# Sliding-window attention followed by a two-matmul expert layer: from 768-token units to 256-token granules with half-array attention tiles

## The chip, the cores and the metric

The kernel runs on one core of one Trainium2 chip. The metric is the device time of one execution in microseconds, taken over repeated runs. A profile of one execution goes with each kernel. Its span is about 2 us shorter than the time of the same run.

Engine names in the profile: PE is the matrix engine and PEld its weight loads, DVE the vector engine, ACT the scalar engine (activations), POOL the engine that issues most of the loads here, SP the one that issues the stores.

## The reference

```python
# q, k, v: [4, 8, 768, 64]; n_global = 8, n_local = 96
scores = (q @ k.transpose(0, 1, 3, 2)) / sqrt(64)
rel  = pos[:, None] - pos[None, :]
keep = (pos[None, :] < 8) | ((rel >= 0) & (rel < 96))       # 8 global keys, or the last 96
dist = where(is_global & ~is_local, 96.0, abs(rel))
scores = where(keep, scores - slopes[h] * dist, -1e9)
a = softmax(scores)
x = (a @ v) as [3072 tokens, 512]                           # 4 * 768 tokens, 8 heads * 64
h = x @ w_in                                                # w_in  [512, 2048]
g = s * relu(h)**2 + b
out = g @ w_out                                             # w_out [2048, 512], float32 out
```

The layer after the attention is called the expert below; `x @ w_in` is its first matmul and `g @ w_out` its second. Note that every query looks at its own 128-token block, the block before it, and 8 global keys, and at nothing else.

## The kernel before

The unit of work is a pair of heads over all 768 tokens of one batch entry: 16 units. Queries and keys are loaded with tokens on partitions and transposed on PE. Both heads of a pair share one full-array score matmul, which needs the queries padded with zeros; the eight global keys take two more score matmuls. The probabilities are then the *weights* of the AV matmuls, and V, with a column of ones beside it, streams through: 65 columns, the last of which is the softmax denominator.

```python
ps_sc = ctx.enter_context(tc.tile_pool(name="ps_sc", bufs=4, space=bass.MemoryType.PSUM))
ps_av = ctx.enter_context(tc.tile_pool(name="ps_av", bufs=2, space=bass.MemoryType.PSUM))
ps_h = ctx.enter_context(tc.tile_pool(name="ps_h", bufs=2, space=bass.MemoryType.PSUM))
# ... prologue(ip): two DMAs each for q, k, v of this head pair ...
        nc.gpsimd.memset(v_ex2[:, :, :, D : D + 1], 1.0)          # the ones column, on POOL
# ... scores of block t: 128 keys against two blocks of zero-padded queries, both heads (L298)
                    ps[:, 0:ncol],                                # ncol = 512
                    lhsT=kP[:, t * P : (t + 1) * P],
                    rhs=zq[:, t : t + (2 if ncol == 4 * P else 1), :],
# ... AV (L373): 480 of these, lhsT = 128x128 probabilities, rhs = 65 columns of V
                            nc.tensor.matmul(ps_pair[:, dr, :], lhsT=lhsT, rhs=rhs, ...)
                    nc.vector.reciprocal(rec[:], ps_pair[:, :, D : D + 1])
                    nc.vector.scalar_tensor_tensor(out=xn[...], in0=ps_pair[:, :, 0:D],
                        scalar=sqrt_s[:], in1=rec[:]..., op0=ALU.mult, op1=ALU.mult)
# ... at the end of a batch entry: x is transposed for the expert
    def x_transpose_stage(bb):
        for kc in range(KC):
            pt = ps_h.tile([P, SB * P], BF16, tag="psh")
            for tb in range(SB):
                nc.tensor.transpose(pt[:, tb * P : (tb + 1) * P], ...)          # L403
            nc.vector.tensor_copy(xT_all[kc][:, bb * S : (bb + 1) * S], pt[:])  # L408
# ... expert, first matmul (a batch entry behind), 384 tokens a PSUM bank
                ps = ps_h.tile([P, 512], F32, tag="psh")
                for kc in range(KC):
                    nc.tensor.matmul(ps[:, 0:clen], lhsT=w_in_bf[:, kc, ...],   # L420
                        rhs=xT_all[kc][:, tok0 + cs0 : tok0 + cs0 + clen], ...)
                nc.scalar.activation(gT_all[...], ps[:, 0:clen], ACT.Relu)      # L427
            nc.vector.tensor_tensor(gs, gs, gs, ALU.mult)                       # L433
# ... expert, second matmul: 512 columns of w_out (L441), add of b, store
```

The expert of a batch entry runs between the attention of the next one. So PE can do no expert work until the attention of all four head pairs of the first entry is through.

The softmax here doesn't subtract the row's maximum and nothing guards it: scores larger than these inputs give would overflow.

## Time and profile before

| | before |
|---|---|
| time | 287.1 us, median of the first three runs; 288.6 over all 15 |
| profiled span | 285.8 us |
| PE busy | 246.2 us (86%) |
| PE work by steady spacing (below) | 225.7 us |
| of it done in the first 57 us | 19.1 us |

The opening of the page, with its slice rows (each digit is one fortieth of the span, 7.1 us, in tenths of busy time), and the shares of the chain of work that ended last:

```profile
span 285.8 us, 4714 instructions
PE 246.2 (86%) x1787; PEld 137.1 (48%) x1808; DVE 160.8 (56%) x471; ACT 147.7 (52%) x299; POOL 88.4 (31%) x132
...
PE   0476087799999999799999997999999999999994
...
DMA  6999999999908696942929252400001111000111
...
PE 76%; POOL 7%; ACT 6%; DMA 5%; DVE 3%; issue 1%; ACTq 0%; POOLq 0%
```

PE is the bound, but not from the start: for eight slices (57 us) it is partly idle while the DMA engines, which carry the loads, stand at nine tenths. The chain's pieces in the first 60 us (start, length, what) show the reason:

```profile
40.02 3.92 DMA k_pair<-in_k_dram
44.08 0.80 PE ps_k L254 x6
...
55.83 2.04 PE ps L420 x12
```

The first expert matmul (L420) starts at 55.8 us. The windows view cuts the span at 57 us (columns: window in us, its length, then busy time and instruction count of PE, PEld, DVE, ACT and POOL, then the granted clock, the DMA share and GB/s):

```profile
0.00:57.00 57.00, 28.86 (x270) 18.71 (x275) 35.59 (x122) 39.31 (x82) 42.53 (x68) 0.88 1.51 135
57.00:286.00 229.00, 217.36 (x1518) 118.37 (x1533) 125.26 (x350) 108.36 (x219) 45.90 (x64) 1.00 0.46 55
```

The groups of instructions, kept apart by form (line, engine, operation, output and inputs, shapes, count | busy us, mean ns | idle time before them and what ended it):

```profile
L420 PE MATMUL ps<-xT,w_in_bf 128*128 128x384 bf16 x512 | 91.3, 325 | 1.7 <-ACT gT_all L427 1.2 <-ACT zq L276 0.4 <-DVE xT L408 0.2
L441 PE MATMUL po<-w_out_bf,gT_all 128*128 128x512 bf16 x376 | 86.3, 379 | 0.4
L427 ACT ACTIVATE gT_all<-ps 128x384 bf16<-128x384 f32 x128 | 62.7, 490 | 42.6 <-PE ps L420 42.6
```

Two cautions on reading them. "128*128" is the part of the array that the matmul uses. And the mean of a matmul (325 ns) is its latency: matmuls overlap, so what counts for a busy PE is the distance from one start to the next. The steady distances in the traces are 216 ns for 512 columns, 162 for 384, 109 for 256, 55.5 for 128, and 30 for 65. "PE work" in this document is the number of matmuls of each form times these distances. In the first expert matmul every eighth start (57 of the 512 matmuls) comes 250 to 260 ns after the last instead of 162: a tile takes four matmuls, only two PSUM buffers (`ps_h`) are there, and so after each two tiles the next has to wait for a 490 ns ReLU. The waits view of PE's weight loads shows the same (line waited in, what for: total us, times, longest):

```profile
PEld L420 <- issue: 10.9, 61, 0.8
```

### The profile page before, as it was taken

The numbers are of one execution on the slowest core, as the hardware profiler recorded it, in microseconds if no ns is written. First come the engines' busy times: TensorE is split into PE (matmuls) and PEld (weight loads), VectorE is DVE, ScalarE is ACT, GpSimd is POOL, SyncE is SP. The second block draws the span as 40 slices with busy tenths as digits, with TensorE's granted clock in tenths as the row PEclk, the third lists the DMA queues.
The fourth block names the chain that finished last, engine by engine and source line by source line (L and its number), as shares of the span: only waits on it lengthen the run. The fifth ranks groups of instructions, "written<-read, shape, count | busy, mean of one in ns | idle before, by whom it ended". The sixth has DMA issues, their size and how long they took to land.

```text
span 285.8 us, 4714 instructions
## 1 busy us (share of the span) xinstructions
PE 246.2 (86%) x1787; PEld 137.1 (48%) x1808; DVE 160.8 (56%) x471; ACT 147.7 (52%) x299; POOL 88.4 (31%) x132
## 2 busy tenths in 40 slices
PE   0476087799999999799999997999999999999994
PEld 0253055455555554555554544655554555555441
DVE  4378357963649283975465656956392836333221
ACT  6888356673575142875680606865760503774000
POOL 9996568397605152503342020200000000000000
PEclk9999667999999999999999999999999999999999
DMA  6999999999908696942929252400001111000111
GB/s 40 120 118 149 177 161 138 175 173 107 92 1 59 103 104 105 78 28 17 69 17 104 75 64 76 28 2 0 2 0 73 40 73 39 0 0 2 73 73 73
DMA packets 81717, 20.22 MB, mean 71 GB/s; under 512 B 76064, under 2 KB 78112, under 8 KB 81696
## 3 DMA queue, kind: packets, MB, share of 16 engines
q0 software_dynamic: 77952, 13.64, 60.8%
q1 hardware_dynamic: 3744, 6.29, 5.9%
q8 instruction: 14, 0.23, 0.3%
q14 instruction: 7, 0.06, 0.1%
HBM read 27.26 MB, written 6.29 MB: 117 GB/s over the span
## 4 chain that ended last, share of the span: by engine, by line
PE 76%; POOL 7%; ACT 6%; DMA 5%; DVE 3%; issue 1%; ACTq 0%; POOLq 0%
PE ps L420 31%; PE po L441 29%; DMA k_pair<-in_k_dram 5%; PE ps L298 5%; PE ps_pair L373 4%; ACT pt L309 3%; POOL q_pair L228 3%; POOL k_pair L232 2%; PE psg L323 2%; POOL v_ex L238 2%; ACT zq L276 1%; PE ps_k L254 1%; PE pt L403 1%; PE ps_cs L195 1%; PE ps_q L262 1%
## 5 line engine op out<-in xcount | busy, mean ns | idle before, releaser
L420 PE MATMUL ps<-xT,w_in_bf 128*128 128x384 bf16 x512 | 91.3, 325 | 1.7 <-ACT gT_all L427 1.2
L441 PE MATMUL po<-w_out_bf,gT_all 128*128 128x512 bf16 x376 | 86.3, 379 | 0.4
L427 ACT ACTIVATE gT_all<-ps 128x384 bf16<-128x384 f32 x128 | 62.7, 490 | 42.6 <-PE ps L420 42.6
L309 ACT ACTIVATE pt<-ps 128x512 bf16<-128x512 f32 x96 | 46.2, 576 | 59.2 <-PE ps L298 54.9
L420 PEld LDWEIGHTS <-w_in_bf 128*128 128x128 bf16 x512 | 48.8, 96 | 39.4 <-issue 10.9
L433 DVE TENSOR_TENSOR gT_all<-gT_all 128x768 bf16<-128x768 bf16 x64 | 35.7, 558 | 43.3 <-ACT gT_all L427 42.9
L441 PEld LDWEIGHTS <-gT_all 128*128 128x128 bf16 x384 | 35.9, 98 | 39.1 <-DVE gT_all L433 0.2
L449 DVE TENSOR_TENSOR o_sb<-po,bvec_rep 128x512 f32<-128x512 f32 x24 | 16.5, 689 | 47.9 <-PE po L441 47.9
L238 POOL DMA_DIRECT2D v_ex<-in_v_dram x32 | 26.8, 862 | 31.8 <-issue 31.8
L232 POOL DMA_DIRECT2D k_pair<-in_k_dram x32 | 27.5, 862 | 27.4 <-PE ps L298 18.2
L312 DVE TENSOR_TENSOR pt<-pt,bmp 128x512 bf16<-128x512 bf16 x96 | 33.8, 394 | 1.8 <-ACT pt L309 1.5
L298 PE MATMUL ps<-zq,kP 128*128 128x512 bf16 (+1 forms) x84 | 29.6, 400 | 3.7 <-ACT zq L276 2.8
L384 DVE SCALAR_TENSOR_TENSOR xnat<-ps_pair,sqrt_s,rec 128x128 bf16<-128x128 f32 x96 | 30.8, 346 | 1.0
L373 PE MATMUL ps_pair<-v_ex,pt 128*128 128x65 bf16 x352 | 28.5, 198 | 3.0 <-DVE xnat L384 2.8
L373 PEld LDWEIGHTS <-pt 128*128 128x128 bf16 x352 | 23.0, 100 | 16.8 <-DVE xnat L384 8.6
L254 PE MATMUL ps_k<-ident_bf,k_pair 128*128 128x128 bf16 x96 | 12.1, 241 | 21.8 <-DMA k_pair<-in_k_dram 21.7
L228 POOL DMA_DIRECT2D q_pair<-in_q_dram x32 | 27.5, 866 | 0.7 <-PE ps_pair L373 0.4
L254 PEld LDWEIGHTS <-k_pair 128*128 128x128 bf16 x96 | 8.6, 107 | 28.2 <-issue 22.9
L331 ACT ACTIVATE pgt<-psg 128x512 bf16<-128x512 f32 x32 | 18.4, 651 | 1.1 <-PE psg L323 1.1
L373 PE MATMUL ps_pair<-v_ex,pgt 128*128 128x65 bf16 x128 | 18.7, 196 | 0.0
L383 DVE RECIPROCAL rec<-ps_pair 128x2 f32<-128x2 f32 x96 | 13.6, 160 | 6.4 <-PE ps_pair L373 5.9
L276 ACT COPY zq<-ps_q 64x768 bf16<-64x768 bf16 x16 | 12.7, 793 | 8.1 <-DVE zq L272 4.9
(42 smaller groups left out, 145.3 us busy)
## 6 DMA issues: line engine op xcount, KB each, us to landing
out_dram<-o_sb SPq DMA_DIRECT2D x24, 256.0 KB, 2.0
q_pair<-in_q_dram POOLq DMA_DIRECT2D x32, 96.0 KB, 3.7
k_pair<-in_k_dram POOLq DMA_DIRECT2D x32, 96.0 KB, 3.6
v_ex<-in_v_dram POOLq DMA_DIRECT2D x32, 96.0 KB, 3.6
w_in_bf<-in_moe_w_in_dram POOLq DMA_DIRECT2D x4, 512.0 KB, 8.1
w_out_bf<-in_moe_w_out_dram POOLq DMA_DIRECT2D x4, 512.0 KB, 8.6
s_bc<-in_moe_s_dram SPq DMA_DIRECT2D x1, 0.5 KB, 2.9
b_bc<-in_moe_b_dram SPq DMA_DIRECT2D x1, 0.5 KB, 3.5
```

The costliest lines, as they stand in the source:

```text
L228: nc.gpsimd.dma_start(q_pair[:, :, hi, :], q[bb, h0 + hi].rearrange("(sb p) d -> p sb d", p=P),)
L232: nc.gpsimd.dma_start(k_pair[:, :, hi, :], k[bb, h0 + hi].rearrange("(sb p) d -> p sb d", p=P),)
L238: nc.gpsimd.dma_start(v_ex2[:, :, hi, 0:D], v[bb, h0 + hi].rearrange("(sb p) d -> p sb d", p=P),)
L298: lambda t=t, ps=ps, ncol=ncol: nc.tensor.matmul(ps[:, 0:ncol], lhsT=kP[:, t * P : (t + 1) * P], rhs=zq[:, t : t + (2 if ncol == 4 * P els ...
L309: nc.scalar.activation(pt[:, 0:ncol], ps[:, 0:ncol], ACT.Exp, scale=QSCALE)
L312: nc.vector.tensor_tensor(pt[:, 0:ncol], pt[:, 0:ncol], bm[:, 0:ncol], ALU.mult)
L373: nc.tensor.matmul(ps_pair[:, dr, :], lhsT=lhsT, rhs=rhs, start=(i_mm == 0), stop=(i_mm == len(mms) - 1),)
L384: nc.vector.scalar_tensor_tensor(out=xn[:, r0 : r0 + 2, hh * D : (hh + 1) * D], in0=ps_pair[:, :, 0:D], scalar=sqrt_s[:], in1=rec[:].to_br ...
L420: nc.tensor.matmul(ps[:, 0:clen], lhsT=w_in_bf[:, kc, fc * P : (fc + 1) * P], rhs=xT_all[kc][:, tok0 + cs0 : tok0 + cs0 + clen], start=(kc ...
L427: nc.scalar.activation(gT_all[:, fc, cs0 : cs0 + clen], ps[:, 0:clen], ACT.Relu,)
L433: nc.vector.tensor_tensor(gs, gs, gs, ALU.mult)
L441: nc.tensor.matmul(po[:, 0:DM], lhsT=gT_all[:, fc, tb * P : (tb + 1) * P], rhs=w_out_bf[:, fc, :], start=(fc == 0), stop=(fc == FC - 1),)
```

## The change

The intent is to get PE to the expert earlier and to keep it there. It is a rewrite of the schedule; the diff is cut to the parts that matter.

- The unit is 256 tokens of a head pair (48 units; a "granule" is 256 tokens of all heads). Loads go by granule, so that the first granule's expert can start long before the batch entry is loaded.
- Scores and AV use half of the array per head. Scores use 64 rows (64\*128); AV uses 64 columns (128\*64) with V as the weights and the probabilities streaming, so that the result comes out as [head dim, tokens], which the expert needs: no transposes of x.
- The denominators are extra matmuls with a block of ones as weights; their reciprocal is exp(-ln(sum)) on ACT.
- The global keys are copied into the tile of the previous block's keys (`koff`, `voff`), so they need no matmul of their own.
- All eight PSUM banks form one pool; ReLU and square work on 512 columns.
- The order of the steps is fixed by hand: two units per step, first matmul of granule j−1, second of j−2.

```diff
-    ps_sc = ctx.enter_context(tc.tile_pool(name="ps_sc", bufs=4, space=bass.MemoryType.PSUM))
-    ps_av = ctx.enter_context(tc.tile_pool(name="ps_av", bufs=2, space=bass.MemoryType.PSUM))
-    ps_h = ctx.enter_context(tc.tile_pool(name="ps_h", bufs=2, space=bass.MemoryType.PSUM))
+    ps_all = ctx.enter_context(tc.tile_pool(name="ps_all", bufs=8, space=bass.MemoryType.PSUM))
+    ps_sc = ps_av = ps_h = ps_all
 ... loads, in this order
+    load_granule(0, 0)
+    load_granule(0, 1)
+    for i in range(4):
+        load_w_in(i, 4)
+    load_granule(0, 2)
+    for i in range(4):
+        load_w_out(i, 4)
 ... scores (L267)
-            mm_ops.append(lambda ...: nc.tensor.matmul(ps[:, 0:ncol],
-                    lhsT=kP[:, t * P : (t + 1) * P], rhs=zq[:, t : t + 2, :]))
+            for kt, kc0, qc0, oc in plan:           # 4 pairs of blocks, 3 in granule 0
+                for hi in range(2):
+                    r0 = hi * D
+                    nc.tensor.matmul(
+                        pss[hi][:, oc * P : (oc + 1) * P],
+                        lhsT=kt[r0 : r0 + D, kc0 : kc0 + P],
+                        rhs=t[r0 : r0 + D, qc0 : qc0 + P], start=True, stop=True)
 ... AV (L315), then the denominators (L328)
+                    for hi in range(2):
+                        nc.tensor.matmul(
+                            av[hi * D : (hi + 1) * D, i * P : (i + 1) * P],
+                            lhsT=vv, rhs=pts[hi][:, c * P : (c + 1) * P], ...)
+                    for hi in range(2):
+                        nc.tensor.matmul(
+                            av[hi * D : (hi + 1) * D, GT + i * P : GT + (i + 1) * P],
+                            lhsT=ones_bf[:, 0:D], rhs=pts[hi][:, c * P : (c + 1) * P], ...)
 ... norm, straight into xT
-                    nc.vector.reciprocal(rec[:], ps_pair[:, :, D : D + 1])
-                    nc.vector.scalar_tensor_tensor(...)
-    def x_transpose_stage(bb): ...
+            nc.scalar.activation(lg[:], av[:, GT : 2 * GT], ACT.Ln)               # L338
+            nc.scalar.activation(rc[:], lg[:], ACT.Exp, scale=-1.0)               # L340
+            nc.vector.tensor_tensor(xT[j][:, hp, :], av[:, 0:GT], rc[:], ALU.mult)  # L341
 ... first expert matmul (L354): two groups of 256 columns a bank, then one ReLU of 512 (L362)
 ... main loop
+    for s in range(0, NSTEP, 2):
+        ...                    # scores of units s+2, s+3; AV and ones of s, s+1
+        if 1 <= jm <= NJ:
+            for i in range(2):
+                moe_p1(jm - 1, 2 * qd + i)
+        if 2 <= jm:
+            moe_p2(jm - 2, qd // 2, 0)
+            moe_p2(jm - 2, qd // 2, 1)
+        if s + 4 < NU:
+            run_T2(s + 4)      # transposes of q and k
+        if 1 <= jm <= NJ:
+            for i in range(2, 4):
+                moe_p1(jm - 1, 2 * qd + i)
```

## The prediction

> **What bounds it now.** The page gives PE 86% busy, and the chain of waits is 76% PE: 31% the first expert matmul (L420), 29% the second (L441). The 40-slice view splits the run. For the first 57 us PE is 51% busy (28.9 us, windows view), while DMA slices stand at 9 and POOL issues 0.86 us per load; then PE is 217 of 229 us busy. Busy time flatters PE, so I used spacing between matmul starts (trace): L441 216 ns (512 columns), L420 162 ns (384 columns), with every fourth about 251 ns, since two PSUM buffers make PE wait for the 490 ns ReLU; attention-times-V (65 columns) 30 ns; 128-column transposes 55 ns. Summed at those steady rates, PE needs 83 (second) + 83 (first) + 26 (scores) + 14 (AV) + 16 (transposes) + 3.5 (bias) = about 226 us. The other 60 us is loading (about 35), ReLU waits (about 8), and attention chains and batch ends (about 17).
>
> **What changes.** The unit becomes 256 tokens instead of a 768-token batch. AV is computed transposed (tokens as columns), so the output transposes (L403, 5 us PE; L408, 8.7 us DVE) go. Zero-padded queries and separate global-score matmuls go too. The denominator becomes extra ones-matmuls, then Ln and Exp on ACT. All eight PSUM banks form one pool, so the ReLU wait should go.
>
> **PE cost after (estimates from the spacings above).** Second expert matmul unchanged, 83; first 768 x 109 = 84 (the 256-column score matmuls here were spaced 109 ns); transposes 192 x 55 = 10.5; bias 3.5. Attention becomes 1056 matmuls of 128 columns in half-array tiles: 59 us if each takes 55 ns alone, 30 us if pairs overlap fully. [...]no tiled matmul is in this trace. So I expect little overlap for the 704 column-tiled ones and some for the 352 row-tiled ones: about 50 us, against 46 for the same work before. PE total about 231, hardly less than before. **The gain is idle PE time, not less PE work.**
>
> **Other engines.** From traced durations: ACT about 158 us (exp 54, ReLU 58, Ln+Exp 40, templates 6), DVE about 155 us. Per two-unit step: 6.5 and 7 us against PE's 8.5 to 9.5; PE stays the bound.
>
> **Start-up.** Six loads per granule at about 1.1 us of POOL each; weight quarters about 2.65 us each (the landing spacing here). Granules 0 and 1 land by about 18 us, w_in by 29, granule 2's keys and queries at about 32, w_out by 45. PE's order puts granule 2's transposes inside the first expert work, so PE is dense from about 32 us, not 57, with 11 us of work done. Then 220 us of PE work,[...] 3 us of tail: 260; I shade it to 258 for partial overlap.
>
> **Prediction:** 258 us, range 243 to 274. Faster by over 2%: 0.95; within 2%: 0.04; slower: 0.01.
>
> **What would show it.** 40 slices: PE at 9 from about 32 us to the end. Groups by form: first expert matmul without the ReLU wait; tiled matmul spacing near 55 ns (no overlap) or 28 ns (overlap). Waits: ACT and DVE waiting for PE.
>
> **What would make it wrong.** Tiled weight loads exposed (100 ns per matmul adds 45 us); full overlap (20 us less); ACT's Ln/Exp or DVE's queue delaying the next scores; loads slower than estimated.

Two passages are cut from this text: one about tiled matmuls, and one term of the sum, about 5 us for losses between matmuls. The sum came to 260 us with that term: 32 us until PE is dense, 220 us of PE work left (231 less the 11 done), the 5 us, and 3 us of tail. The 50 us for attention lies between two limits that follow from the 55 ns of the trace (59 and 30 us); its place between them was the author's estimate and no measurement. The other unit costs come from the trace of before: 1.1 us of POOL a load is about the 0.86 us of a 96 KB load times 128/96, for the size of a load after the change; 2.65 us is the distance at which quarters of w_out landed (50.53 and 53.18 us, 59.46 and 62.11 us); 100 ns is the mean of a weight load (96 to 107 ns), and 1056 × (100 − 55.5) ns is 47 us.

## The result

| | before | after |
|---|---|---|
| time, median (range) | 288.6 us (286.9–291.0, 15 runs) | 248.4 us (246.8–249.2, 12 runs) |
| profiled span | 285.8 us | 246.1 us |
| PE work by steady spacing | 225.7 us | 210.3 us |
| PE work done by 57 us | 19.1 us | 31.0 us |

The ratio is 0.860, with a 95% interval of 0.857 to 0.863. Ratios in this document are the mean time of one kernel's fast runs over that of the other's of the same rounds, so they are not quite the ratio of the medians. Executions over 1.5% slower than the fastest of the same kernel are left out of the means.

The page of after, same rows as before:

```profile
span 246.1 us, 5897 instructions
PE 227.8 (93%) x2393; PEld 158.7 (64%) x2416; DVE 150.8 (61%) x449; ACT 131.5 (53%) x297; POOL 70.8 (29%) x89
...
PE   0588699999999999999999999999999999999993
...
DMA  6999999999994012999011001101101101100112
...
PE 85%; POOL 6%; DMA 5%; issue 1%; DVE 1%; POOLq 0%
```

Slices are 6.2 us here, so PE is at nine tenths from about 31 us on. Two pieces of the chain of work that ended last, and the windows, cut at 57 us again:

```profile
16.64 12.70 DMA knat<-in_k_dram
...
29.68 1.07 PE ps L354 x5
```

```profile
0.00:57.00 57.00, 43.97 (x481) 30.75 (x484) 33.73 (x114) 34.21 (x75) 42.71 (x57) 0.97 1.76 160
57.00:246.00 189.00, 183.87 (x1913) 127.94 (x1932) 117.03 (x336) 97.28 (x222) 28.10 (x33) 1.00 0.50 59
```

The groups that answer to those of before (L354 is the first expert matmul, L388 the second, L362 the ReLU), and the new ones-matmuls:

```profile
L354 PE MATMUL ps<-xT,w_in_bf 128*128 128x256 bf16 x768 | 93.7, 276 | 0.0
L388 PE MATMUL ps<-w_out_bf,gT 128*128 128x512 bf16 x362 | 85.5, 379 | 1.2
...
L362 ACT ACTIVATE gT<-ps 128x512 bf16<-128x512 f32 x96 | 57.2, 620 | 95.3 <-PE ps L354 95.3
...
L328 PE MATMUL ps_av<-pt,ones_bf 128*64 128x128 bf16 x352 | 20.1, 230 | 0.0
...
L328 PEld LDWEIGHTS <-ones_bf 128*64 128x64 bf16 x352 | 14.2, 117 | 0.3 <-issue 0.2
```

No wait for the ReLU is left in the first expert matmul, and from 57 us on its starts within a run are 109 ns apart. ACT waits for PE (95 us in all), not PE for ACT. (L388 ran 384 times, as its weight loads show; 22 of its matmul records are missing, and one more elsewhere. The PE work of 210.3 us counts them.)

The surprise is in the timeline of PE. This is part of the AV and the denominators of two units (start, length, line, array part, shape, count):

```profile
88.52 0.22 PE L315 MATMUL ps_av<-pt,voff 128*64 128x128 bf16 x2
88.58 0.22 PE L315 MATMUL ps_av<-pt,vnat 128*64 128x128 bf16 x2
88.64 0.22 PE L315 MATMUL ps_av<-pt,voff 128*64 128x128 bf16 x2
88.69 0.39 PE L328 MATMUL ps_av<-pt,ones_bf 128*64 128x128 bf16 x8
...
89.14 0.39 PE L328 MATMUL ps_av<-pt,ones_bf 128*64 128x128 bf16 x8
89.46 1.05 PE L354 MATMUL ps<-xT,w_in_bf 128*128 128x256 bf16 x8
```

Read the starts of the two heads' pairs: 88.52, 88.58, 88.64, 88.69; and eight ones-matmuls take 88.69 to 88.91, where the next AV matmul starts. Each *pair* takes 56 ns, 28 per matmul. The records in the trace start 3 to 4 ns and then 52 to 53 ns apart. That is full overlap of the two halves of the array.

### Where the 39.7 us came from

The difference of the profiled spans can be split with PE's work alone, because PE is the bound: span = PE work + idle before 57 us + idle after.

| | before | after | gain |
|---|---|---|---|
| PE work | 225.7 | 210.3 | 15.4 |
| 57 us less the work done by then | 37.9 | 26.0 | 11.9 |
| the rest of the span less the rest of the work | 22.2 | 9.8 | 12.4 |

So some 40% of the gain is less PE work, and the prediction had said that there would be hardly any. The attention of after costs PE about 1056 × 28 ns = 30 us at the steady spacing (over all its starts after 57 us the mean is 30 ns); the same work cost 26 (scores) + 14 (AV) + 5 (transposes of x) before.

### The profile page after: what moved, and what is told of

Same layout as the page of the kernel before. It is cut to its first block, busy times and chain, and to the rows that moved or that the text cites. A ratio compares the mean times of both kernels' runs of the same rounds, so it can differ in the third digit from the quotient of the medians.

```text
span 246.1 us, 5897 instructions
## 1 busy us (share of the span) xinstructions
PE 227.8 (93%) x2393; PEld 158.7 (64%) x2416; DVE 150.8 (61%) x449; ACT 131.5 (53%) x297; POOL 70.8 (29%) x89
## 4 chain that ended last, share of the span: by engine, by line
PE 85%; POOL 6%; DMA 5%; issue 1%; DVE 1%; POOLq 0%
PE ps L354 35%; PE ps L388 33%; DMA knat<-in_k_dram 5%; PE ps_av L315 5%; PE ps_s L267 4%; PE ps_av L328 4%; PE ps_t L203 2%; PE ps_t L211 2%; POOL knat L79 2%; POOL qnat L79 1%; POOL vnat L79 1%; PE ps_b L370 1%; POOL w_in_bf L91 1%; DVE o_sb L397 0%; DVE koff L226 0%
## 5 line engine op out<-in xcount | busy, mean ns | idle before, releaser
L362 ACT ACTIVATE gT<-ps 128x512 bf16<-128x512 f32 x96 | 57.2, 620 | 95.3 <-PE ps L354 95.3
L354 PE MATMUL ps<-xT,w_in_bf 128*128 128x256 bf16 x768 | 93.7, 276 | 0.0
L388 PE MATMUL ps<-w_out_bf,gT 128*128 128x512 bf16 x362 | 85.5, 379 | 1.2
L354 PEld LDWEIGHTS <-w_in_bf 128*128 128x128 bf16 x768 | 73.4, 99 | 11.4 <-issue 0.2
L388 PEld LDWEIGHTS <-gT 128*128 128x128 bf16 x384 | 37.6, 98 | 40.6
L363 DVE TENSOR_TENSOR gT<-gT 128x512 bf16<-128x512 bf16 x96 | 40.6, 423 | 23.8 <-ACT gT L362 21.2
L277 ACT ACTIVATE pt<-ps_s 128x512 bf16<-128x512 f32 (+1 forms) x96 | 46.1, 574 | 4.9 <-PE ps_s L267 4.9
L281 DVE TENSOR_TENSOR pt<-pt,tmpl 128x512 bf16<-128x512 bf16 (+1 forms) x96 | 38.3, 404 | 4.5 <-ACT pt L277 0.3
L79 POOL DMA_DIRECT2D knat<-in_k_dram x24 | 21.6, 915 | 30.1 <-PE ps_t L211 25.6
L341 DVE TENSOR_TENSOR xT<-ps_av,rc 128x256 bf16<-128x256 f32 x48 | 18.7, 419 | 10.1 <-ACT rc L340 10.1
L221 DVE COPY qk<-ps_t 128x512 bf16<-128x512 bf16 x48 | 18.0, 414 | 6.6 <-PE ps_t L211 6.6
L203 PE MATMUL ps_t<-ident_bf,knat 128*128 128x128 bf16 x96 | 13.7, 237 | 8.8 <-DMA knat<-in_k_dram 8.8
L79 POOL DMA_DIRECT2D qnat<-in_q_dram x24 | 21.5, 918 | 0.2
L328 PE MATMUL ps_av<-pt,ones_bf 128*64 128x128 bf16 x352 | 20.1, 230 | 0.0
L203 PEld LDWEIGHTS <-knat 128*128 128x128 bf16 x96 | 8.6, 104 | 14.1 <-DMA knat<-in_k_dram 9.4
```

What stands on the lines that cost most here:

```text
L79: nc.gpsimd.dma_start(t[:, sb, h0 : h0 + nh, :], src[b, h0 : h0 + nh, sb * P : (sb + 1) * P, :].rearrange("h p d -> p h d"),)
L203: lambda i=i: nc.tensor.transpose(ps[:, (GB + i) * P : (GB + i + 1) * P], kn[:, g * GB + i, 2 * hp : 2 * hp + 2, :], ident_bf[:],)
L277: nc.scalar.activation(pts[hi][:, 0:ncol], pss[hi][:, 0:ncol], ACT.Exp, scale=QSCALE)
L281: nc.vector.tensor_tensor(pts[hi][:, 0:ncol], pts[hi][:, 0:ncol], m, ALU.mult)
L328: nc.tensor.matmul(av[hi * D : (hi + 1) * D, GT + i * P : GT + (i + 1) * P], lhsT=ones_bf[:, 0:D], rhs=pts[hi][:, c * P : (c + 1) * P], st ...
L354: nc.tensor.matmul(ps[:, i, :], lhsT=w_in_bf[:, kc, fc * P : (fc + 1) * P], rhs=xT[j][:, kc, :], start=(kc == 0), stop=(kc == KC - 1),)
```

## Experiments

Twelve kernels ran. The questions were: does the overlap of the halves carry the 15 us (theory), or would matmuls of 128 columns in the whole array have done as well (rival: only the schedule matters)? What is the PSUM pool worth, in each kernel? What sets the start before and after?

### The overlap of the halves

**a_serial.** All matmuls of head 0 before those of head 1, within a unit. Runs of four in one half.

```diff
-            for kt, kc0, qc0, oc in plan:
-                for hi in range(2):
+            for hi in range(2):
+                for kt, kc0, qc0, oc in plan:
```
(and the same in AV and in the ones-matmuls)

> The changed kernel with the same 1056 half-array attention matmuls, but all of one head first and then all of the other, so that neighbours use the same half of the array. If neighbours in different halves overlap (starts 3 ns and 52 ns apart in the changed kernel's trace), each of the 528 pairs loses about 50 ns: 26 us more, about 274 us, and every start is 52 ns or more after the last. If the spacing is set by weight loads or issue and not by overlap, the time stays within 2 us of 248.

Measured: 249.1 us, ratio to before 0.861 against 0.860 for after. By the expectation's wording that would mean that overlap plays no part. But the trace says otherwise: the edit did not do what it was for. PE's timeline of this kernel:

```profile
88.73 0.26 PE L315 MATMUL ps_av<-pt,vnat 128*64 128x128 bf16 x2
88.81 0.23 PE L315 MATMUL ps_av<-pt,voff 128*64 128x128 bf16 x2
```

The program has vnat, voff, vnat, voff of head 0, and then the same four of head 1. The trace has two vnat matmuls starting together, then two voff: the second head's matmuls were started beside the first head's, ahead of their place in the program. In this trace the two halves thus run like two streams, and a run of four in one half does not hold the other half back.

**a_long.** Runs of up to 16 in one half: head 0 of both units of a step, then head 1 of both.

```diff
-        def mms():
+        def mms(hi):
 ... (no loop over hi inside)
+        # in the step: scores of both units for hi = 0, then for hi = 1; AV and ones likewise
```

> As a_serial, which did not slow the kernel because the two halves still ran side by side with runs of four matmuls in one half; here runs of up to 16 matmuls stay in one half (scores of two units, then AV and denominators of two units). If the engine looks only a few matmuls ahead, the halves stop overlapping and it takes up to 26 us longer, about 270. If it looks 16 ahead (32 instructions with the weight loads), no change, 248 to 250.

Measured: 264.9 us, ratio 0.923, which is 16 to 18 us more than after (from the medians, and from the difference of the ratios). PE's timeline in the middle of a step:

```profile
93.37 0.39 PE L328 MATMUL ps_av<-pt,ones_bf 128*64 128x128 bf16 x4
93.59 0.22 PE L315 MATMUL ps_av<-pt,vnat 128*64 128x128 bf16 x1
...
93.82 0.22 PE L328 MATMUL ps_av<-pt,ones_bf 128*64 128x128 bf16 x1
93.82 0.24 PE L315 MATMUL ps_av<-pt,vnat 128*64 128x128 bf16 x1
```

Within a run the starts are 55 ns apart. Only at 93.82, when four of head 0's sixteen are left, does head 1 start beside them. So the reach is short: four matmuls with their weight loads, read at this seam, which agrees with a_serial. An estimate from that reach: 48 attention matmuls a step, with two seams of four pairs, take 48 × 55.5 − 2 × 4 × 55.5 = 2.2 us instead of 48 × 28 = 1.3; over 22 steps' worth (1056 / 48) that is 19 us, near the 16 to 18 measured. The starts of the attention matmuls summed over the trace agree: 54.1 us in a_long against 35.0 in after (each distance counted up to 150 ns). The overlap is thus real time, not an artefact of modelled ends.

**a_full.** Every attention matmul uses the whole array: both heads' rows or columns as weights. The mathematics is wrong (it mixes two heads; the comparison with the reference did not notice it, so its tolerance would not catch such a mistake); counts and streamed columns are the same.

```diff
-                        lhsT=kt[r0 : r0 + D, kc0 : kc0 + P],
-                        rhs=t[r0 : r0 + D, qc0 : qc0 + P],
+                        lhsT=kt[:, kc0 : kc0 + P],
+                        rhs=t[:, qc0 : qc0 + P],
 ... AV and ones: all 128 columns, heads accumulated into one tile
```

> The changed kernel with all 1056 attention matmuls made full-array (both heads' rows or columns at once; the result is wrong on purpose), so that no two can run side by side. If the half-array tiles are worth what the trace's spacing says (28 ns per matmul on average against 55 ns), this adds 1056 times 27 ns: about 28 us, 276 us. If the spacing is set by weight loads or issue (the full-array 65-column matmuls of the kernel before were 30 ns apart), the time stays near 249.

Measured: 268.3 us, ratio 0.932, about 20 us more than after (28 had been expected). PE's timeline:

```profile
86.71 0.61 PE L328 MATMUL ps_av<-pt,ones_bf 128*128 128x128 bf16 x8
87.16 0.28 PE L315 MATMUL ps_av<-pt,vnat 128*128 128x128 bf16 x2
...
87.61 0.61 PE L328 MATMUL ps_av<-pt,ones_bf 128*128 128x128 bf16 x8
88.05 0.71 PE L354 MATMUL ps<-xT,w_in_bf 128*128 128x256 bf16 x5
```

Eight matmuls take 0.45 us instead of 0.22. This refutes the rival: the same schedule with the same instructions on the whole array loses half of the gain. The 20 us are less than 1056 × (55.5 − 28) = 29 us. About 6 us of the difference is visible: in after, each change of array mode (attention tiles to expert tiles and back) leaves a gap of about 0.1 us beyond the steady spacing, 0.35 us a step, 5.9 us over the 17 steps after 57 us; here, where the mode never changes, these gaps are 0.02 us in all after 57 us. In the lines above, ones to L354 is 0.44 us for eight matmuls, no gap; in after (89.14 to 89.46) it is 0.32 us where eight take 0.22. The other 3 us lie at the start: counted at 55.5 ns a matmul, a_full has 33.9 us of work done by 57 us against 31.0 in after, so that part of the longer attention fell into time in which PE of after waits for loads.

### PSUM pools

**a_split.** After with before's pools (4, 2 and 2 banks).

```diff
-    ps_all = ctx.enter_context(tc.tile_pool(name="ps_all", bufs=8, ...))
-    ps_sc = ps_av = ps_h = ps_all
+    ps_sc = ctx.enter_context(tc.tile_pool(name="ps_sc", bufs=4, ...))
+    ps_av = ctx.enter_context(tc.tile_pool(name="ps_av", bufs=2, ...))
+    ps_h = ctx.enter_context(tc.tile_pool(name="ps_h", bufs=2, ...))
```

> The changed kernel with the eight PSUM banks cut 4/2/2 as in the kernel before (scores/attention output/everything else). If the shared pool is what removed the ReLU wait, PE waits for ACT's ReLU again in the first expert matmul: 6 to 12 us more, 254 to 260 us. If the 512-column ReLU for eight matmuls (0.87 us of PE against about 0.87 us of round trip) and the finer interleaving removed it, under 2 us more.

(The round trip in it is an estimate. In the trace of after the median from the start of a tile's last matmul to the end of its ReLU is 0.91 us.)

Measured: 269.1 us, ratio 0.931: 20.5 us more than after (0.0710 × 288.6), where 6 to 12 had been expected. The longest of PE's waits (L389 is the second expert matmul here, L363 the ReLU):

```profile
PE ps L389 <- ACT gT L363: 11.0, 18, 0.8
```

Each turn from the first to the second expert matmul must now wait until one of two banks is free of its ReLU of 620 ns. From the distances of the starts after 57 us, these turns cost 13.3 us.

The edit also did something that its lines do not say. The source's order of steps is unchanged, but the built program has PE's instructions in another order: nine attention matmuls of each step now stand ahead of the expert's (L212 is a transpose, L316 AV, L329 the ones, L355 the first expert matmul here).

```profile
100.81 0.28 PE L212 MATMUL ps_t<-ident_bf,qnat 128*128 128x128 bf16 x2
101.02 0.25 PE L316 MATMUL ps_av<-pt,vnat 128*64 128x128 bf16 x2
...
101.48 1.91 PE L355 MATMUL ps<-xT,w_in_bf 128*128 128x256 bf16 x16
```

In after the transposes are followed by the expert matmuls directly. So PE changes the array mode oftener (35 turns from attention to expert after 57 us instead of 18), and these gaps cost 4.8 us more. The two together are 18 of the 20.5 us.

The pool was worth more than the prediction's 8 us, because in the new schedule both expert matmuls and the transposes take turns on what are now two banks. The new schedule thus does not get its time with the cut of before. Another fixed cut, with three banks for the expert as in b_h3 below, was not run on it.

**b_shared.** Before with one pool of eight.

```diff
-    ps_sc = ...bufs=4...; ps_av = ...bufs=2...; ps_h = ...bufs=2...
+    ps_all = ctx.enter_context(tc.tile_pool(name="ps_all", bufs=8, space=bass.MemoryType.PSUM))
+    ps_sc = ps_av = ps_h = ps_all
```

> The kernel before with one pool of eight PSUM banks for everything. If its two banks for the expert matmuls caused the ReLU wait, every fourth first-expert matmul no longer stands out (251 to 162 ns) and it is 7 to 10 us faster, about 279 us. If its waits come from the attention chain and the batch ends, under 2 us.

Measured: 285.6 us, ratio 0.990 (0.982 to 0.997), which is neither of the two expectations. Summed over the trace after 57 us, the excess of the starts in the first expert matmul over the steady spacing fell from 7.0 to 0.7 us. But that between AV matmuls rose from 0.4 to 9.6 us. Of this, 9.1 us are 39 gaps that end about 50 ns after ACT finishes an exp of a score tile: with one ring of buffers, a small AV tile takes its turn behind larger tiles that are still being read. Here too the built order of PE changed: the 30 AV matmuls of a unit stand in one block, where before has many of them spread among expert matmuls. The same pool removed the wait and made a new one; what is left of the gain lies before 57 us (21.9 us of work done by then against 19.1).

**b_h3.** Before with one bank moved from the scores to the expert: 3, 2, 3.

```diff
-    ps_sc = ...bufs=4...
+    ps_sc = ...bufs=3...
-    ps_h = ...bufs=2...
+    ps_h = ...bufs=3...
```

> The kernel before with PSUM cut 3/2/3 instead of 4/2/2: a third bank for the expert matmuls and transposes, without the common ring of b_shared, in which the attention-times-V tiles waited instead. If the ReLU wait is a matter of two against three banks, its 7 us go (first-expert matmuls all about 162 ns apart) and the run takes about 281 us. If a bank less for scores costs as much, 285 to 289.

Measured: 280.6 us, ratio 0.968 (0.962 to 0.974), a gain of 9 us. The group of the first expert matmul and the waits of its weight loads:

```profile
L420 PE MATMUL ps<-xT,w_in_bf 128*128 128x384 bf16 x512 | 86.1, 326 | 0.3 <-DVE xT L408 0.2
```

```profile
PEld L420 <- issue: 0.8, 4, 0.3
```

Against 91.3 us busy and a wait of 10.9 us before. The sum of the start distances in L420 fell from 91.2 to 84.4 us, and the work done by 57 us did not change (18.9 us). So 7 to 9 of the 12.4 us of later idle time are the ReLU wait, and one line takes them away in the old kernel as well. The remaining 3 to 5 us (attention chains and the ends of batch entries) I did not separate.

### What sets the start

In before, POOL issues all loads, and in its waits stands the line below: it waits for V to land before it may write the ones column. Three kernels test whether this holds the start back.

```profile
POOL v_ex L242 <- DMA v_ex<-in_v_dram: 34.3, 13, 3.8
```

**b_bufs**: eight load buffers instead of four (`bufs=8` in the pools of q, k and v). **b_memset**: the ones column written by DVE before V is loaded, so that POOL never waits for V:

```diff
         v_ex2 = ldv.tile([P, SB, 2, D + 1], BF16, tag="vex")
+        nc.vector.memset(v_ex2[:, :, :, D : D + 1], 1.0)
 ... two loads of V
-        nc.gpsimd.memset(v_ex2[:, :, :, D : D + 1], 1.0)
```

**b_load**: both.

> The kernel before with eight instead of four load buffers for q, k and v. If its late dense start (57 us) comes from loads held back until PE frees a buffer (POOL waited 27 us for PE in all), dense work starts some 4 us earlier and the run is 3 to 6 us faster. If the start is set by the transfers themselves and by the 768-token unit, no change (under 1.5 us).

> The kernel before with the ones column of V written by DVE ahead of the V loads, instead of by POOL behind them. In the kernel before POOL, which issues all loads, waited 34 us for V to land before that memset, and the loads behind it waited too. If that holds back the start, the first expert matmul begins 3 to 5 us earlier and the run is 3 to 6 us faster. If the transfers themselves are the limit, under 1.5 us.

> b_memset with eight load buffers as in b_bufs, so that POOL waits neither for V to land nor for PE to free a buffer. If both waits hold the loads back, one standing in for the other in the single edits, this is 4 to 8 us faster than the kernel before. If the transfers or the 768-token unit set the start, under 1.5 us.

Measured: 288.3, 288.5 and 287.8 us; ratios 0.997, 1.001 and 0.999, and each interval holds 1. The first expert matmul began at 55.9, 56.0 and 57.1 us, against 55.7 in before. In b_load the loads are issued earlier, yet they land at the same time. Its chain, to be set beside the chain of before (40.02 and 44.08):

```profile
36.32 7.91 DMA k_pair<-in_k_dram
44.36 0.50 PE ps_k L254 x6
```

The key load is on its way for 7.9 us instead of 3.9 and ends at 44.2 us, against 43.9. So neither the waits of POOL nor the buffers set the start of before. What is left is the transfers themselves, together with the order in which PE's program needs them (no run changes these in before): the keys of the sixth unit, which come behind the loads of five units and all of w_in, are transposed ahead of the first expert matmul. This supports the change's way of gaining the start, by loading less before the first expert matmul, and it shows that a long wait in the table need not be worth anything.

**a_order.** After, with the third granule loaded right behind the first quarter of w_in, because the chain of after holds a transfer of 12.7 us, that granule's keys. (PE itself stood still for only 2.0 us of it, in two waits before L203.)

```diff
     load_granule(0, 1)
-    for i in range(4):
-        load_w_in(i, 4)
+    load_w_in(0, 4)
+    load_granule(0, 2)
+    for i in range(1, 4):
+        load_w_in(i, 4)
-    load_granule(0, 2)
     for i in range(4):
         load_w_out(i, 4)
```

> The changed kernel with granule 2's loads moved ahead of the last three quarters of w_in. In the changed kernel PE stood at granule 2's transposes until 29.7 us. If that wait is the start-up limit, about 6 us faster, 243. If the next limit is right behind it (w_out lands whole at 42.7 us and the bias matmuls that need all of it began at 43.5 us), under 1.5 us faster.

Measured: 245.6 us, ratio 0.848, about 3 us less than after, between the two expectations. Part of it goes with the clock: all four runs have a granted clock of 0.996 to 0.998, and the three runs of after with 0.997 or more took 246.9 us on average. At equal clock the gain is thus about 1.3 us (an estimate from these runs). The chain then waits for the next thing in the queue:

```profile
25.11 17.90 DMA w_out_bf<-in_moe_w_out_dram
...
43.05 1.02 PE ps_b L371 x4
```

**a_order_lag.** Also the second expert matmul one granule later (three behind instead of two, with a third buffer of its input), so that PE has attention and first-matmul work while w_out comes in; the first granule of the second batch entry is loaded ahead of w_out for this.

```diff
-    gpool = ...bufs=2...
+    gpool = ...bufs=3...
-    NSTEP = NU + 2 * HP
+    NSTEP = NU + 3 * HP
-        if s == 2 * HP:
+        if s == 3 * HP:
             emit_bvec()
-        if 2 <= jm:
-            moe_p2(jm - 2, qd // 2, 0)
+        if 3 <= jm:
+            moe_p2(jm - 3, qd // 2, 0)
```

> a_order, with the second expert matmul one granule later (three gT buffers) and the next batch's first granule loaded ahead of w_out, so that PE has attention and first expert matmuls to do while w_out comes. If the start is set by which bytes PE's order asks for first, PE has some 5 us more work done at 57 us and the run takes 243 to 245 us. If it is set elsewhere, 248 to 250.

Measured: 243.5 us (243.0 to 244.4), ratio 0.841, about 5 us less than after. The work done by 57 us rose from 31.0 us (after) to 33.8 (a_order) and 35.7 (a_order_lag). This is the best version; it beats both kernels. Against the same three runs of after the gain is about 3.4 us.

### The reciprocal

**a_recip.** After with DVE's reciprocal in place of Ln and Exp on ACT.

```diff
-            nc.scalar.activation(lg[:], av[:, GT : 2 * GT], ACT.Ln)
-            nc.scalar.activation(rc[:], lg[:], ACT.Exp, scale=-1.0)
+            nc.vector.reciprocal(rc[:], av[:, GT : 2 * GT])
```

> The changed kernel with the denominator's reciprocal as one DVE instruction of 128x256 instead of Ln and Exp on ACT. [...]DVE stays under PE and the time is 247 to 250. [...]DVE passes PE and it takes 260 us or more, which would show why the change gave it to ACT.

(Its two conditions are cut, because they gave rates of DVE that no trace shows: the 247 to 250 us were expected if the reciprocal is cheap, the 260 or more if it is dear. DVE's multiplication over a 128x256 tile, L341 in after, took 419 ns.)

Measured: 254.9 us, ratio 0.880, about 6 us more than after and between the two expectations (247 to 250, and 260 or more). The reciprocal in the groups, and the engines' busy times:

```profile
L338 DVE RECIPROCAL rc<-ps_av 128x256 f32<-128x256 f32 x48 | 83.6, 1745 | 0.1
```

```profile
PE 228.9 (90%) x2393; PEld 159.1 (63%) x2416; DVE 214.1 (84%) x497; ACT 108.1 (43%) x201; POOL 70.9 (28%) x89
```

One reciprocal of 128x256 takes 1745 ns, 6.8 ns per column, where Ln and Exp take 428 + 461 ns. In before the reciprocal was taken of two columns at a time (160 ns), because the denominator stood once per token; transposed AV puts it into all 64 rows of a head, and so makes the detour over ACT worth it. DVE does not become the bound throughout, though: most of the loss is at the start, where 26.1 us of work are done by 57 us instead of 31.0. There PE waits for DVE's copies of the transposed queries and keys (L221), before which DVE has the reciprocals to do; in after the same wait is 1.6 us:

```profile
PE ps_s L267 <- DVE qk L221: 9.6, 4, 3.8
```

After 57 us the idle time of PE is only 2.4 us longer than in after. (The detour costs no table loads between Ln and Exp: after has a single one, 1283 ns (L65), in the whole span.)

## Why the prediction was right or wrong

The time, 248.4 us, lies in the range (243 to 274), and the direction was right. Point by point:

- **"PE stays the bound": right.** PE went from 86% to 93% busy and from 76% to 85% of the chain; DVE was 150.8 us busy (predicted 155), ACT 131.5 (predicted 158). ACT's figure was too high by a fifth, which did not matter.
- **"PE is dense from about 32 us": right.** The slice row stands at 9 from about 31 us. The first expert matmuls run at 24.6 us instead of 55.7, then PE stands at the transposes of granule 2 (28.4 and 29.4 us) until their keys land. Its worth was less than implied: the prediction gave 11 us as the work done by about 32 us (measured: 8.8, although a load took 0.9 us of POOL and not the 1.1 assumed), and 25 us more dense work would have made 36 by 57 us. Measured: 31.0. So 2 of the missing 5 us were missing at 32 us already; the rest is short idle time after that. a_order and a_order_lag raise the figure to 33.8 and 35.7.
- **"The ReLU wait should go": right**, and worth 7 to 9 us in the old kernel (b_h3; 8 had been said). In the new schedule the split of banks of before costs 20.5 us, of which 13.3 are the wait for the ReLU and 4.8 come from a changed order of PE (a_split); that the new schedule needs the banks that much more had not been seen.
- **"I expect little overlap for the 704 column-tiled ones ... about 50 us": wrong.** This is the mis-sized term: attention on PE measured about 30 us, not 50. From it came "PE total about 231, hardly less than before", and **"the gain is idle PE time, not less PE work"**: 15.4 of the 39.7 us were less PE work. The step that failed was to expect that the weight loads of tiled matmuls would be exposed; it was the author's estimate, and no trace had shown it. Loads of 64 columns took 117 ns (L328) where loads of 128 columns took 99 (mean of the weight loads of L354 in the same groups, not copied above), so they are slower per column. But the loads run beside the matmuls, and nothing of them shows: 28 ns a matmul where the halves alternate, and in a_long, where one half works alone, 55 ns, not the 100 that the prediction named as a risk. a_full and a_long show that the overlap is worth 16 to 20 us net.
- **The cut term of about 5 us for losses between matmuls: about right**, though no trace had shown it. The gaps at the changes of array mode alone are 5.9 us after 57 us, about 0.1 us each.
- The sum, term by term: PE work was predicted as 231 us and measured 210.3; idle time was predicted as 29 us (32 − 11 = 21 at the start, 8 later, of which 5 are the cut term) and measured 35.8 (26.0 and 9.8). So 260 − 20.7 + 6.8 = 246.1, which is the profiled span. Two errors of opposite sign put the 258 closer than its parts were; that much of the agreement was luck.

Open: why a change of array mode costs 0.1 us; how far the reach of four matmuls holds for other forms than these; the part of the 12.4 us that is not the ReLU wait; how the 11.9 us at the start divide between the smaller unit and the order of loads, which no run separates; and how much of the gain at the start is the clock, which was granted at 0.88 before 57 us in the kernel before and at 0.97 in after (windows view), since no run changes the clock alone. An estimate from the spread of the runs: within the runs of before and of after, a run with 0.01 less mean clock is 1.1 to 1.3 us longer, and the means are 0.970 and 0.990, so about 2 of the 40 us go with the clock.

## What to carry to other kernels

Two independent half-size matmuls (64 rows or 64 columns) in the two halves of the array can run at the price of one (here 56 ns a pair), if they alternate within about four matmuls in the program; count them at half the spacing before deciding that a tiled form is no gain. A pool of buffers is right or wrong for an order of work: the same eight-bank pool was worth 20 us in one schedule and 1% in the other, where moving a single bank gave 3%. When you change buffers, compare the order of the built program too: here it changed with them. When loading bounds the start, first ask what the first large piece of work needs and load that first; waits of the issuing engine may be worth nothing (three kernels showed 0%).
